# A written-out order of 1,999 operations: the same operations, all behind the first 278 in a newly drawn order

## The chip, the core and the metric

One core of one Trainium2 chip runs the whole kernel. The metric is the time of one execution in device microseconds, as the median of several runs. The profile is that of one execution, taken by the hardware profiler; it has a time of its own, and the span from its first to its last recorded event is somewhat shorter.

The engines are named as in the profile: PE (TensorE, matrix products), DVE (VectorE), ACT (ScalarE), POOL (GpSimd) and SP, whose queue issues most DMA transfers. Each engine works through its own queue in order. An instruction that waits holds up all that stands behind it in that queue.

## The reference

Attention over blocks of keys that each query selects, then a gated feed-forward layer. Four batches, eight heads, 768 positions of 64 features; 3,072 tokens, 512 features, 1,536 hidden ones.

```python
k_min, k_max = np.min(k_chunks, axis=3), np.max(k_chunks, axis=3)      # chunks of 32 keys
ub = sum_d max(q * k_min, q * k_max)                                   # a bound for each chunk
ub = np.where(causal, ub, -1e9)
top_chunks = np.argsort(ub, axis=-1)[..., -6:]
scores = q @ k.T / sqrt(64), masked to the top chunks and to earlier keys
attn = softmax(scores) @ v
x = attn as (3072, 512)
out = (sigmoid(x @ w_gate) * (x @ w_val)) @ w_out
```

## The kernel before, in words

The kernel describes its work as 1,999 named operations. `Plan.add` takes for each its engines, what it reads and writes, and the code that emits its instructions. A text, `ORDER`, then lists all names once. `Plan.order` reads it word by word: `name@ENGINE:slots` gives the engine (without `@`, the first of those that the operation allows) and the slot of every buffer that the operation is the first to hold. The instructions are emitted in that order, so the words of one engine, in their order, are that engine's queue, and a buffer that gets an occupied slot has to wait until the last reader of its former owner is done. The order between words of different engines has no effect by itself. Words are counted from 0 here.

The tokens are cut into units of up to three blocks of 128 queries. Unit u0 takes the first blocks of three batches, which need no selection; u1 to u7 the rest. For each unit:

- Loads. q and k of batch 0 come as wide tiles; for batches 1 to 3 as four transfers each (`load_blocks`, L568: k00, k01, k10, k11 and the same for q, 384 KB each), into one of two buffers of the kind `big`. v comes as one transfer per block (L581) into six buffers. A buffer is free for the next batch when all that reads it is done.
- Keys (L754): for each pair of heads p, `kx0`, `kx1` take minimum and maximum, `k16` casts, `kt` transposes, `hk0`, `hk1` spread the halves. Queries: `qf` transposes on DVE (L781), `qm` takes the positive part, `hq0`, `hq1` cast.
- Selection (L802): `ub` computes the bounds on PE, `ubn` transposes them, `mx` finds the sixth largest, `ap` compares, `apt` transposes back, and `hqm` copies the result into the rows of the query tile that carry the mask.
- Attention (L860): `sc` are score products in up to three banks per head, `exp` the exponential on ACT, `cm` the causal mask (POOL or DVE), `pv` the product with v, `rz` and `x` the normalisation on DVE. `xT` turns x by a DMA transpose on SP's queue (from u3 on; before by `xps` on PE).
- Feed-forward (L953) for u0 to u3: `g` and `v` products of four matmuls each, `tanh` on ACT, `hg` on DVE, three groups `o0`, `o1`, `o2` per block, `osb` and the store `out`.
- The units 4 and 5, and 6 and 7, are taken as pairs (`ffn_pair`, L1039; `project_pair`, L1185), with seven products where eight would be plain. `Sg`, `Sv`, `So` are sums of weights, `T0` to `T3` of inputs; `P1` to `P7` are the products, `E` copies a bank, `C` adds a bank to the copy, `hg` gates; `S1` to `S4` are sums for the output side, on DVE or POOL, `Q1` to `Q7` its products, `F` and `G` bring them into the output tile. This is called the pair stage below.

PSUM has eight banks, given out by the slots of the kind `ps`. `beat` are filler transposes on PE at the start.

Of the kernel before, what the change touches and what calls it, by code (L numbers as in the profile page):

```python
# [102 lines left out]
qT_u1_3:6 kxf1:1 kf1_1 hk1_u1_3@ACT hq0_u1_1@POOL k2_u2 qf_u1_2 vf1_1:1 kn_u1_2@DVE:0 beat3:7 qfT_0:2 qf_u1_3 qf0_1:0
kxf0 kT_u1_2:1 hq0_u1_3@POOL qf1_1 qf16_0:4 v10 qm_u1_2@ACT:0 vf_1:0 hk0_u1_1 qf_u1_0 after4 qf_u2_3@DVE:1 kf16_0:0
kcr_f kx0_u1_3 hkq101@POOL vf_2:1 beat4:7 scf_0:0,4,1 after2 vf1_3:2 kfT_1:3 expf_0_1:2 kn_u2_2@DVE:4 expf_0_0 hkf1
kx0_u1_2 beat5:7 kT_u2_2:4 qf0_2:3 kx1_u1_3 kf16_1:3 q2_u2 ident16 qm_u1_3@ACT beat6:7 qfT_1:0 cmf_0_0@DVE qf1_2
v16_0_0@ACT cmf_0_1@DVE kx1_u1_2 qf16_1:4 kf1_2:0 beat7:7 pvf_0_0:3 hq0_u1_0 rzf_0_0:0 k1_u2 beat8:7 scf_1:0,5,1
xf_0_0:0 kx1_u2_2:1 kf0_2 expf_1_0 xpsf_0_0:3,0 kt_u1_2@DVE:0 k3_u2 after6 expf_1_1:3 vf1_2:3 hk0_u1_3 k0_u2
qm_u1_0@ACT after5 vc_1@DVE wv0 qm_u1_1@ACT kx0_u2_2 q1_u2 hq1_u2_3 hk0_u1_2@POOL v_0_3:2 hkf0@ACT beat9:7 qfT_2:5 wg0
cmf_1_0@DVE pvf_0_1:1 v_0_2:1 xTf_0_0@ACT qn_u2_2@DVE:0 qf16_2@DVE:4 kn_u2_1:5 wg1 beat10:7 qT_u2_2:3 pvf_1_0:0  # L110
cmf_1_1@DVE beat11:7 kfT_2:5 kcr_u1 wv1 rzf_1_0:0 xf_1_0:0 kf16_2:0 rzf_0_1:1 wg2 hkq010 kn_u2_3:6 xf_0_1:1 beat12:7
scf_2:5,0,1 pvf_1_1:2 hk1_u1_2@POOL ub_u1:1,6 expf_2_1:2 rzf_1_1:1 wv2 xf_1_1:2 expf_2_0 cmf_2_1@DVE vc_2@ACT
cmf_2_0@DVE xpsf_1_1:5 xpsf_1_0:2 kT_u2_1:0 hq1_u1_2@POOL ubn1_u1:0 qf_u2_2 pvf_2_0:7 v_0_1:0 qm_u2_2@ACT:0 xpsf_0_1:3
hq1_u1_1@POOL rzf_2_0:1 pvf_2_1:6 xTf_1_0@ACT kx0_u2_1 kt_u2_2:0 kn_u2_0@POOL:3 xf_2_0:1 beat13:2 kT_u2_3:2 qn_u2_1:5
rzf_2_1:0 wo0 xTf_1_1@ACT xpsf_2_0:7 xf_2_1:0 kt_u2_1:1 qn_u2_0@DVE:6 beat14:4 xpsf_2_1:6 xTf_0_1@ACT ubn0_u1
qT_u2_1:5 hq0_u1_2@POOL xTf_2_0@ACT qT_u2_0:4 kx0_u2_3 xTf_2_1@ACT v_u0_2:1 hkp111@POOL kx1_u2_3 hkp000@ACT vb_u0_2
kt_u2_3@DVE:2 v_u0_1:6 ubm0_u1 mx0_u1:0 hk0_u2_3@POOL vb_u0_1 hkp010@ACT v_u0_0:2 wo1 vb_u0_0 ap0_u1 v_u0_3:7
# [5 lines left out]
sc_u1_3_1:3,3 tanh_u0_7 g_u0_5:6,3,6 kx0_u2_0 tanh_u0_6 kx1_u2_0 sc_u1_2_0:5 hq1_u1_3@DVE tanh_u0_5 kcr_u2@POOL
kt_u2_0@DVE:2 exp_u1_3_1 v16_0_3@DVE hq1 apt1_u1 hg_u0_2 g_u0_4:7,0,7 sc_u1_3_2:6 v_u0_6:0 v_u0_7:3 hqm1_u1_0 v_u0_4:2
tanh_u0_4 hg_u0_7 hq1_u1_0@POOL exp_u1_2_2 v_u0_5:7 exp_u1_2_0 hg_u0_4 hq1_u2_2 ub_u2:4,3 cm_u1_2@DVE exp_u1_3_2
hg_u0_5 hkq110@ACT sc_u1_3_0:7 ubn1_u2:0 g_u0_10:6,3,8 exp_u1_3_0 hqm1_u1_2@DVE g_u0_11:3,0,9 hg_u0_6 ubn0_u2
g_u0_8:0,1,10 mx0_u2:0 sc_u1_1_1:4 g_u0_9:7,2,11 exp_u1_1_1 ap0_u2 v16_0_2@DVE v_u0_8:4 tanh_u0_9 kcr1 apt0_u2:0
# [20 lines left out]
kt_1_2:0 qf16_3:4 sc_u2_5_0:5,1 v_u1_1:1 exp_u2_4_1 x_u2_0:0 g_u1_5:3,0,1 exp_u2_5_0 qf0_u3_0:1 kf16_3:3 sc_u2_5_1:2
hk1_1_0@DVE sc_u2_3_1:5 k11_2 v_u1_5:0 vc_3 qf0_u3_1 exp_u2_3_1 qf0_u3_2 sc_u2_5_2:6 exp_u2_4_2 v_u1_6:5 qf0_u3_3
exp_u2_5_1 xps_u2_0:7 cm_u2_5@DVE v_u1_8:4 tanh_u1_5 qm_u3_0@POOL:0 qf0_u4_2:0 k00_2 qm_u3_2@ACT hg_u1_5 pv_u2_3:3  # L150
pv_u2_2 exp_u2_5_2 xT_u2_0 qf0_u4_1 g_u1_6:7,0,2 hg_u1_8 hk1_1_1 scf_3:6,0,3 rz_u2_1:0 pv_u2_4:4 x_u2_1:0 expf_3_0
k10_2 pv_u2_5 g_u1_1:3,3,3 expf_3_1:0 cmf_3_0@DVE rz_u2_2:0 ub_u3:6,2 cmf_3_1 qf0_u4_3 tanh_u1_1 x_u2_2:1 tanh_u1_6
hq1_u3_0@POOL hg_u1_1 hk1_1_3@ACT v_1_2:0 hg_u1_6 pvf_3_1:7 pvf_3_0:1 hk1_1_2 xps_u2_1:4 o0_u1_0:3,0 rzf_3_1:0
out_u0_2 xf_3_1:0 rzf_3_0:1 hk0_1_2 v_2_1:2 ubn0_u3:0 o1_u1_0 qf0_u4_0 ubm0_u3 k16_2_0@ACT:0 xf_3_0:2 k16_2_3:2
q01_2:0 o2_u1_0 xT_u2_1 mx0_u3:0 k16_2_2@ACT:5 hq0_u3_2@POOL xpsf_3_1:4 o0_u1_1:1,1 ubn1_u3 ap0_u3 xps_u2_2:2 ubm1_u3
v16_1_2 xpsf_3_0:6 apt0_u3:0 o1_u1_1 xT_u2_2@ACT xTf_3_1 xTf_3_0@ACT hq0_u3_0@POOL mx1_u3 hqm0_u3_0@ACT o2_u1_1 q10_2
# [1252 lines left out]
```

## Time and profile before

| | us |
|---|---|
| median of three runs | 282.03 (281.38 to 282.8) |
| the profiled execution | 282.25 |
| its span | 280.2 |
| PE busy | 268.8 |
| DVE busy | 246.8 |
| ACT busy | 220.4 |
| POOL busy | 134.6 |

A row of the stretches gives, for each engine, its busy microseconds and in brackets its instructions. In the timeline a row has its start, its length, the engine, the line and what is written from what; what stands in square brackets at its end is how long the engine had been idle before and what it had waited for. "x4" at the end of a row of the chain or the timeline means that four instructions that follow each other were merged. PE's matmuls overlap, so a matmul's own length is longer than the step from one to the next.

### The profile page before, as it was taken

To read this page: it belongs to the slowest core of one execution; us is meant where nothing else is said; L and a number is where in the kernel's file an instruction comes from. 1 tells how busy PE (TensorE), PEld (TensorE's weight loads), DVE (VectorE), ACT (ScalarE), POOL (GpSimd) and SP (SyncE) were. 2 spreads that over 40 slices of the span, in tenths; PEclk is the share of its full clock that TensorE was granted. 3 is DMA by queue.
4 is the path that set the end of the run, shared out by engine and by line. 5 is a ranking of instruction groups with operands and counts; after the bars stand their busy time and mean duration, and the time that the engine had idled before them with its cause. 6 is when DMAs were issued, how large, how long until landed. Compare 5 with 4: busy or idle time off the path is not lost.

```text
span 280.2 us, 7449 instructions
## 1 busy us (share of the span) xinstructions
PE 268.8 (96%) x2758; PEld 186.3 (67%) x2758; DVE 246.8 (88%) x679; ACT 220.4 (79%) x474; POOL 134.6 (48%) x206
## 2 busy tenths in 40 slices
...
PEclk9999999999999999999999999999999999999999
...
DMA packets 131699, 34.68 MB, mean 124 GB/s; under 512 B 119760, under 2 KB 128720, under 8 KB 131664
## 3 DMA queue, kind: packets, MB, share of 16 engines
...
HBM read 30.67 MB, written 6.29 MB: 132 GB/s over the span
## 4 chain that ended last, share of the span: by engine, by line
PE 83%; DVE 5%; ACT 4%; DMA 3%; issue 2%; SPq 1%; POOL 0%; ACTq 0%; DVEq 0%
PE sc_u L876 12%; PE g_u L968 11%; PE v_u L968 10%; PE o_u L1006 10%; PE pv_u L912 6%; PE suo_u6u L1233 3%; PE suo_u4u L1233 3%; PE sug_u4u L1092 3%; PE suv_u4u L1092 3%; PE sug_u6u L1092 2%; PE suv_u6u L1092 2%; PE ube_u L814 2%; DMA k<-in_k_dram 2%; DMA kq_u<-in_q_dram 1%; PE sro_u4u L1233 1%
## 5 line engine op out<-in xcount | busy, mean ns | idle before, releaser
L887 ACT ACTIVATE att_u<-sc_u 128x512 f16<-128x512 f32 (+3 forms) x184 | 90.9, 549 | 15.1 <-PE sc_u L876 12.7
L896 POOL TENSOR_SCALAR_AFFINE_SELECT att_u<-att_u 128x384 f16<-128x384 f16 (+1 forms) x48 | 26.8, 570 | 44.0 <-ACT att_u L887 42.8
L968 PE MATMUL g_u<-xT_u,wg 128*128 128x384 f16 (+2 forms) x208 | 37.6, 314 | 0.0
L968 PE MATMUL v_u<-xT_u,wv 128*128 128x384 f16 (+2 forms) x208 | 36.4, 313 | 0.0
L1006 PE MATMUL o_u<-wo,hg_u 128*128 128x512 f16 x144 | 35.3, 379 | 0.1
L876 PE MATMUL sc_u<-hqe,hke 128*128 128x128 f16 (+2 forms) x220 | 28.2, 243 | 1.6 <-ACT hqe L359 1.2
L987 DVE SCALAR_TENSOR_TENSOR hg_u<-gate_u,v_u 128x384 f16<-128x384 f16 x48 | 24.8, 538 | 4.7 <-PE v_u L968 3.1
L912 PEld LDWEIGHTS <-att_u 128*128 128x128 f16 x640 | 25.0, 98 | 5.0 <-issue 1.2
L876 PE MATMUL sc_u<-hqo,hko 128*128 128x128 f16 (+2 forms) x220 | 27.9, 243 | 0.0
L912 PE MATMUL pv_u<-v,att_u 128*128 128x65 f16 x640 | 27.0, 193 | 0.0
L982 ACT ACTIVATE gate_u<-g_u 128x384 f16<-128x384 f32 x48 | 22.7, 498 | 5.0 <-PE g_u L968 3.3
L968 PEld LDWEIGHTS <-wv 128*128 128x128 f16 x208 | 19.1, 98 | 10.1 <-issue 0.5
L968 PEld LDWEIGHTS <-wg 128*128 128x128 f16 x208 | 18.9, 98 | 9.5 <-issue 0.2
L876 PEld LDWEIGHTS <-hke 128*128 128x128 f16 x220 | 16.6, 98 | 8.9 <-issue 1.9
L1006 PEld LDWEIGHTS <-hg_u 128*128 128x128 f16 x144 | 13.2, 98 | 11.9 <-issue 0.7
L876 PEld LDWEIGHTS <-hko 128*128 128x128 f16 x220 | 17.0, 98 | 5.8
L931 DVE TENSOR_TENSOR x_u<-pv_u,rz_u 128x384 f16<-128x384 f32 (+1 forms) x28 | 15.0, 534 | 1.2 <-DMA xT_u<-x_u 0.4
L365 POOL CAST v<-v 128x512 f16<-128x512 f32 x15 | 9.1, 612 | 12.9 <-DMA v<-in_v_dram 9.4
L480 PE MATMUL beat<-ident 128*128 128x128 f32 x70 | 12.0, 305 | 1.4 <-POOL ident masks.py:199 1.4
L837 DVE MAX8 mx_u<-ubn_u 128x8 f32<-128x8 f32 (+16 forms) x152 | 12.7, 159 | 0.1
L1092 PEld LDWEIGHTS <-Sg 128*128 128x128 f16 x96 | 9.0, 98 | 5.2
L1092 PEld LDWEIGHTS <-Sv 128*128 128x128 f16 x96 | 9.0, 98 | 5.0 <-issue 0.3
...
## 6 DMA issues: line engine op xcount, KB each, us to landing
...
k<-in_k_dram SPq DMA_DIRECT2D x12, 384.0 KB, 5.7
q<-in_q_dram SPq DMA_DIRECT2D x12, 384.0 KB, 5.8
...
```

The costliest lines, as they stand in the source:

```text
L837: nc.vector.max(at(mx)[:, e_, j, :], at(ubn)[:, e_, j, 0:max(8, u.seen[j])])
L876: nc.tensor.matmul(at(t)[:, o:o + 128 * m], hk[b % 2][e_][:, p, 128 * jb:128 * jb + 128], hq[u.side][e_][:, p, 128 * x:128 * (x + m)], sta ...
L887: plan.add(f"exp_{u.name}_{h}_{y}", {ACT: act(n)}, lambda e, t=t, att=att, b0=b0, n=n: nc.scalar.activation(at(att)[:, b0:b0 + n], at(t), ...
L896: nc.gpsimd.affine_select(out=dv, in_=dv, compare_op=ALU.is_ge, fill=0.0, base=0, pattern=[[0, u.m], [1, 128]], channel_multiplier=-1)
L912: nc.tensor.matmul(at(pv)[:, last, x, :], at(att)[:, c:c + 128], v16[b % 2][:, jb, h, :], start=(jb == 0), stop=(jb == ib))
L931: plan.add(f"x_{u.name}_{p}", {DVE: dve(u.t)}, lambda e: nc.vector.tensor_tensor(at(x_).rearrange("p a (e d) -> p e a d", e=2), at(pv)[:, ...
L968: nc.tensor.matmul(at(t)[:, lo:hi], w16[:, c, 128 * fb:128 * fb + 128], at(u.xt)[:, c, lo:hi], start=(c == 0), stop=(c == 3))
L982: plan.add(f"tanh_{u.name}_{fb}", {ACT: act(T)}, lambda e, g=g, gate=gate: nc.scalar.activation(at(gate), at(g), AF.Tanh, scale=0.5), read ...
L987: plan.add(f"hg_{u.name}_{fb}", {DVE: dve(T)}, lambda e, w_=w_, gate=gate, hg=hg: nc.vector.scalar_tensor_tensor(at(hg), at(gate), 1.0, at ...
L1006: nc.tensor.matmul(at(o), hgs[c][1][1]()[:, 128 * tb:128 * tb + 128], wo16[:, fc, lo:hi], start=(c == 0), stop=(c == NFB - 1))
L1092: nc.tensor.matmul(at(t), left[i](c), right[i](c), start=first and c == 0, stop=c == 1, skip_group_check=not first)
L1233: nc.tensor.matmul(at(t), sums[what[i][0], f][1]()[:, 128 * tb:128 * tb + 128], what[i][1](f), start=first and f == 0, stop=f == half - 1, ...
```

## The change

Only the text `ORDER` differs. It has the same 1,999 names. On each engine the queue is the same up to word 278 or so; there the first difference on PE stands at its 71st operation. Behind it the order is drawn anew, with other engines for 132 operations and other slots for the buffers that 597 words give out. Some lines of it, those with the words that are spoken of:

```diff
--- before.py
+++ after.py
@@ -95,193 +95,194 @@
 BEATS = (14, 9, 4, 3, 8, 1, 3, 2, 1, 10, 2, 1, 4, 2, 2, 4)
 
 ORDER = """
-ident q3_u1:0 epat0:0 k0_u1 tri0 ap1 epat q2_u1 k1_u1 q3_u2:1 q1_u1 q0_u1 kn_u1_0:0 qn_u1_3@DVE:1 ap0 v11 kf1_0:0
...
-exp_u1_5_1 exp_u1_6_0 sc_u1_4_2:2,0 sc_u1_6_1:3 cm_u1_6@DVE k01_1 sc_u1_7_1:4,2 exp_u1_4_2 sc_u1_7_0:6 rz_u1_0:0
...
-kt_1_0:1 v_u1_3:3 cm_u2_7 q11_1:0 sc_u2_6_2:4 g_u1_3:0,0,9 kx0_1_1 hk0_1_0 exp_u2_6_2 v_u1_4:7 tanh_u1_3 kx1_1_3
...
-g_u1_11:7,2,6 hg_u1_2 hg_u1_3 sc_u2_3_2:4,2 v_u1_11:6 exp_u2_3_2 kx1_1_1 tanh_u1_11 qfT_3:3 q10_1 sc_u2_3_0:4 hg_u1_11
...
-exp_u3_6_1 ap0_u4 exp_u3_5_2 v_u2_9:0 k01_3 hq0_u4_0@POOL apt0_u4:0 tanh_u2_9 v_u2_5:3 tanh_u2_10 hg_u2_9 hk1_2_0
...
-sc_u4_2_1:2,0 ub_u5:7,0 k16_3_3@ACT:2 k16_3_2:0 v_2_5:4 hg_u2_10 hg_u2_8 out_u1_2 hqm0_u4_0@ACT hq1_u5_2@POOL pv_u3_4
...
-o2_u3_0 cm_u5_6 exp_u5_4_2 ap1_u6 ub_u7:1,0 exp_u5_4_1 rz_u5_1:1 cm_u5_4 x_u5_1:1 osb_u3_0 hqm0_u6_2 apt1_u6 xT_u5_1
...
-C3g_u4u5_4 P4g_u4u5_5 E0v_u4u5_5:3 P5v_u4u5_4 C0v_u4u5_4 tanh_u4u5_0_11:1 P6v_u4u5_4 cm_u7_7 C0v_u4u5_5 P4g_u4u5_4
...
-P4v_u6u7_4 S4_u6u7_2@POOL hg_u6u7_0_11 Q1_u6u7_1:5,0,7,0 hg_u6u7_0_10 Q1_u6u7_2:1,6,2 C1v_u6u7_4 F0_u6u7_1
...
-F2_u6u7_1 out_u7_1 Q3_u6u7_1 G3_u6u7_0 Q4_u6u7_0 G1_u6u7_1 out_u6_1 F2_u6u7_0 out_u7_0
...
+ident q3_u1:0 epat0:0 k0_u1 beat0:7 tri0 epat q2_u1 ap1 k1_u1 q3_u2:1 q1_u1 qn_u1_3@DVE:1 q0_u1 kn_u1_0:0 ap0 v11
...
+g_u0_7:3,1,4 hq1_u1_0@DVE ap1_u1 hg_u0_1 kT_u2_0:6 sc_u1_3_1:4,2 apt1_u1 hq1_u1_3@POOL kcr1 gb_u0_2 tanh_u0_2 hg_u0_2
...
+k16_1_0@ACT:5 q01_1:0 kf0_3 q00_1 sc_u2_7_0:4 o0_u0_2:1,1 v_u1_5:3 hg_u1_5 o1_u0_2 o2_u0_2 hq0_u2_3 v16_0_5
...
+g_u1_1:1,0,9 exp_u2_2_2 x_u2_0:0 sc_u2_5_2:2 v_u1_1:6 k16_1_2:4 hk1_1_1 kt_1_2:1 q11_1 qf0_u4_2:1 tanh_u1_1 hg_u1_1
...
+kcr_2@POOL tanh_u2_3 hg_u2_3 pv_u3_0:2 ub_u4:4,0 ubn0_u4:0 k00_3:1 qf0_u5_0 pv_u3_1 hk1_1_2@ACT tanh_u2_9
...
+hg_u2_5 k16_3_2@ACT:1 sc_u3_4_1:6 exp_u3_4_1 xT_u3_0:0 v_1_5:3 cm_u3_6 hqm0_u4_0 pv_u3_7:3 v_u2_6:2 k16_3_0@ACT:5
...
+o2_u3_0 cm_u5_7 pv_u5_7 cm_u5_4 pv_u5_4:4 xT_u5_0:0 out_u2_2 x_u5_1:2 xT_u5_1 mx0_u7:0 exp_u6_0_1 Sv1 v16_2_5@DVE Sv3
...
+exp_u6_4_0 o2_u3_2 osb_u3_2 T0_u4u5:0 hk1_3_1@DVE cm_u6_1@DVE ap0_u7 pv_u6_1:0 P5g_u4u5_1:4 mx1_u7 E3g_u4u5_1:6
...
+S2_u4u5_0 hg_u4u5_0_5 P4g_u4u5_4 tanh_u4u5_0_10:0 tanh_u4u5_0_4:2 P3v_u4u5_5 C1v_u4u5_5 cm_u7_2 pv_u7_2:7
...
+tanh_u6u7_1_10:0 P2v_u6u7_5 C0v_u6u7_5 P7g_u6u7_5 C3g_u6u7_5 hg_u6u7_0_5 P5v_u6u7_4 S1_u6u7_3@POOL S3_u6u7_3@POOL
...
+tanh_u6u7_1_11:1 hg_u6u7_1_11 S1_u6u7_4 S1_u6u7_5 Q1_u6u7_1:6,0,1,0 Q1_u6u7_2:3,5,4 F0_u6u7_2 S2_u6u7_4 S4_u6u7_1
...
+S4_u6u7_4 S4_u6u7_5 Q6_u6u7_0 S3_u6u7_5 F3_u6u7_2 F1_u6u7_0@DVE S4_u6u7_3@POOL Q3_u6u7_2 F1_u6u7_2@DVE G1_u6u7_2
...
+out_u6_1 Q4_u6u7_0 F2_u6u7_0@DVE out_u7_0
 """
```

More of the change, by code (lines that the diff above doesn't have):

```diff
@@ L103 @@
[L103 to L117, printed above, removed]
@@ L123 @@
[L123 to L127, printed above, removed]
@@ L148 @@
[L148 to L156, printed above, removed]
-hk0_1_3 kx1_2_0:1 g_u2_4:6,0,12 osb_u1_1 ap1_u3 sc_u3_0_2:4,0 sc_u3_0_0:2 apt1_u3 tanh_u2_4 v_u2_3:1 hqm0_u3_2@DVE
```

322 lines of the change are left out of this document (175 added, 147 removed).

## The prediction

> **What bounds the kernel now.** I read the page first, then the span in seven stretches, then the chain of waits and the timeline at the one stretch that is not full.
>
> ```profile
> span 280.2 us, 7449 instructions
> PE 268.8 (96%) x2758; PEld 186.3 (67%) x2758; DVE 246.8 (88%) x679; ACT 220.4 (79%) x474; POOL 134.6 (48%) x206
> PEclk9999999999999999999999999999999999999999
> PE 83%; DVE 5%; ACT 4%; DMA 3%; issue 2%; SPq 1%; POOL 0%; ACTq 0%; DVEq 0%
> ```
> ```profile
> core 0: us, PE busy (x) PEld busy (x) DVE busy (x) ACT busy (x) POOL busy (x), PEclk, DMA share, GB/s
> 0.00:35.00 35.00, 28.99 (x286) 23.49 (x287) 28.01 (x92) 26.91 (x56) 24.59 (x53) 1.00 1.01 211
> 35.00:120.00 85.00, 84.96 (x890) 55.24 (x889) 74.70 (x221) 66.20 (x141) 37.70 (x60) 1.00 1.04 185
> 120.00:130.00 10.00, 8.35 (x82) 4.16 (x81) 8.94 (x16) 6.42 (x11) 5.39 (x8) 1.00 0.70 150
> 130.00:167.47 37.47, 37.47 (x466) 25.94 (x464) 34.81 (x116) 34.16 (x72) 27.12 (x38) 1.00 0.62 130
> 167.47:212.90 45.43, 45.22 (x512) 30.54 (x512) 43.08 (x111) 43.30 (x95) 21.95 (x30) 1.00 0.13 34
> 212.90:276.80 63.90, 63.78 (x531) 46.94 (x528) 57.28 (x128) 43.00 (x103) 17.85 (x22) 1.00 0.14 48
> 276.80:280.20 3.40, 0.00 (x0) 0.00 (x0) 0.00 (x0) 0.38 (x1) 0.00 (x0) 0.87 0.40 154
> ```
>
> The profiled execution took 282.25 us, 2.05 us outside its span of 280.2; it stands 0.22 us above the median of the three runs, 282.03. TensorE carries 83% of the chain at a full clock. Beyond 35 us it is idle for 0.04 + 1.65 + 0.21 + 0.12 us by these rows, then 3.4 us while the last output leaves. Busy time hides part of a loss, since matmuls overlap in it, so I also count work by steps. The chain gives a step where TensorE follows itself:
>
> ```profile
> 71.46 0.65 PE v_u L968 x4
> 126.66 0.86 PE o_u L1006 x4
> 218.50 0.66 PE suo_u4u L1233 x6
> ```
> ```profile
> L968 PE MATMUL g_u<-xT_u,wg 128*128 128x384 f16 (+2 forms) x208 | 37.6, 314 | 0.0
> L968 PE MATMUL v_u<-xT_u,wv 128*128 128x384 f16 (+2 forms) x208 | 36.4, 313 | 0.0
> L1006 PE MATMUL o_u<-wo,hg_u 128*128 128x512 f16 x144 | 35.3, 379 | 0.1
> L912 PE MATMUL pv_u<-v,att_u 128*128 128x65 f16 x640 | 27.0, 193 | 0.0
> ```
>
> That is 0.163 us for 384 columns, 0.216 for 512, 0.110 for 256, or 0.42 ns a column. With the counts (352 full-width products of L968, 336 of 384 columns in the pair products P, 144 of L1006, 252 of 256 columns in the pair projections Q, 640 of L912 at 0.030, 440 score matmuls of together 82,000 columns, seven bounds at about 1.2 us) the work after 35 us is about 235 us. It stands in 276.8 - 35 = 241.8 us. So some 6.5 us is all that any order of this work could win there, and the largest single piece is here:
>
> ```profile
> 118.57 5.43 DMA k<-in_k_dram
> 124.17 0.78 issue
> ```
> ```profile
> 123.58 1.03 PE L1006 MATMUL o_u<-wo,hg_u 128*128 128x512 f16 x4
> 124.10 0.83 ACT L359 CAST k<-k 128x768 f16<-128x768 f32 x1 [3.03 <-DMA k<-in_k_dram]
> 124.94 0.83 ACT L359 COPY hqe<-apt_u 64x768 f16<-64x768 f16 x1
> 125.83 0.22 PE L876 MATMUL sc_u<-hqe,hke 128*128 128x128 f16 x1 [1.22 <-ACT hqe L359]
> 126.45 0.22 PE L876 MATMUL sc_u<-hqe,hke 128*128 128x128 f16 x1 [0.41 <-ACT att_u L887]
> ```
>
> The last quarter of batch 3's keys, k01_3, is issued at 118.57 and lands at 124.0. ScalarE's cast k16_3_3 stands in front of it for 3.03 us, and behind the cast stands hqm0_u4_0, which the score matmul at 125.83 needs. The projection before it ends its steps at 123.58 + 0.86 = 124.44, so TensorE loses 1.39 us, and 0.57 more ahead of 126.45 (125.83 + 0.05 to 126.45): **2.0 us**.
>
> **What the change does, and what each part costs.** It removes and adds no operation; TensorE's first 70 operations stay, which is 35 us. After that every queue is redrawn, 132 operations change engine and 597 their buffers. I added the durations of before along each queue: TensorE's work stays 258.1 us by steps, DVE's goes from 246.1 to 243.4, ACT's from 219.1 to 213.2, POOL's from 134.6 to 140.9. None passes TensorE in the sum, so the sums alone give no change; what counts is where one queue runs late.
>
> *The wait for k_3: -2.0 us (between 0 and -2.0).* In the new order the four loads follow kx1_2_0, which frees their buffer after 87.7 us of TensorE work, only out_u1_2 between them waiting until 92.6; their first reader k16_3_2 stands at 102.5. The margin is 9.8 to 14.7 us, where before it was 8.4 for k01_3 (released at 101.2 behind v16_2_0, used at 109.6). A load takes
>
> ```profile
> k<-in_k_dram SPq DMA_DIRECT2D x12, 384.0 KB, 5.7
> q<-in_q_dram SPq DMA_DIRECT2D x12, 384.0 KB, 5.8
> ```
>
> to land, so four at half a microsecond of issue each need about 7.7. I take the whole gain.
>
> *A new wait for q_1: +0.3 us (0 to 1.3).* The last loads of batch 1's queries now stand behind qf0_3, which waits for v16_0_4 at 54.8; DVE's qf0_u4_2 wants them at 61.2, a margin of 6.4. Before, the same loads went out like this:
>
> ```profile
> 69.72 0.42 SPq L552 DMA_DIRECT2D qf<-in_q_dram  x1
> 71.17 4.82 SPq L573 DMA_DIRECT2D q<-in_q_dram  x3
> ```
>
> Four issues (qf0_3, q10_1, qf1_3, q11_1) at 0.42 to 0.5 us and 5.8 to land make 7.7: DVE stands some 1.3 us late. Queued behind it are hg_u1_1, four more transposes of q and hg_u1_3. The first TensorE operation that needs one of them is sc_u2_2_1 at 66.0, whose bank hg_u1_1 frees, 4.4 us after hg_u1_1's turn, and DVE has 10 us idle of the 85 before 120. That is the cover; without it the 1.3 us would pass on.
>
> *DVE in the pair stage: +1.1 us (0 to 3.5).* From word 1205 to 1580 (150.8 to 195.2 us of TensorE work) DVE's queue now holds 93 instructions and 45.0 us against 91 and 44.0 before, for the same 44.3 us of TensorE. It gains Sv1, So0, So1, C0v, C1v, a net E, one hg, two cm, two S2, v16_2_5 and hk1_3_1 and gives up Sg0, Sv2, apt1_u6, ubn0, ubn1, an x, two rz and three S3:
>
> ```profile
> L1034 DVE TENSOR_TENSOR Sv<-wv 128x1536 f16<-128x1536 f16 x2 | 1.9, 949 | 0.0
> L1180 DVE TENSOR_TENSOR hko<-wo 128x1536 f16<-128x1536 f16 x1 | 1.0, 952 | 0.0
> L1107 DVE TENSOR_TENSOR c0v_u4u<-c0v_u4u,sqv_u4u 128x384 f32<-128x384 f32 x6 | 3.2, 546 | 0.0
> L848 DVE STREAM_TRANSPOSE apt_u<-ap 128x384 f16<-128x384 f16 (+2 forms) x14 | 7.3, 522 | 0.3
> L825 DVE STREAM_TRANSPOSE ubn_u<-ubo_u 128x384 f32<-128x384 f32 (+2 forms) x7 | 3.7, 534 | 1.2 <-PE ubo_u L814 1.1
> L931 DVE TENSOR_TENSOR x_u<-pv_u,rz_u 128x384 f16<-128x384 f32 (+1 forms) x28 | 15.0, 534 | 1.2 <-DMA xT_u<-x_u 0.4
> ```
>
> Before, DVE was busy for 43.08 of the stretch's 45.43 us, so a microsecond more on it lengthens the stretch by up to 1.055. I take 1.0 x 1.055. Nothing, if its idle 2.35 us can be used; 3.5, if POOL's 27.4 us there (22.6 before) hold DVE up besides. What such a hold-up looks like before:
>
> ```profile
> L1122 DVE SCALAR_TENSOR_TENSOR hg_u<-gate_u4u,c0v_u4u 128x384 f16<-128x384 f16 x6 | 3.7, 625 | 0.0
> L1122 DVE SCALAR_TENSOR_TENSOR hg_u<-gate_u4u,suv_u4u 128x384 f16<-128x384 f16 x6 | 3.1, 542 | 0.0
> ```
>
> The form that reads its second input from a c tile takes 83 ns more than the one that reads it from a bank. Eight such microseconds of hg, and eight of T, S, cm and weight sums, are 16 of DVE's 45; if that share of POOL's added 4.8 us were lost to DVE it would be 1.7 us, and with the order's own 0.95 to 1.5 us the bound is (1.7 + 1.5) x 1.055 = 3.4, rounded up.
>
> [...]
>
> *Closer spacing elsewhere: +1.0 us (0 to 1.6).* Adding each queue's durations up to the operation that makes an input, and TensorE's steps up to the one that needs it, 89 TensorE operations before have their last input less than 0.2 us ahead of their turn; in the new order 120. The 4.5 us that before loses beside k_3 come to 0.05 us for each of the 89, 1.6 us for 31 more; part lies in the pair stage and is counted there.
>
> *The end: nothing.* The last projections (word 1936 on) follow each other as before, and the way out after the last matmul is the same 3.4 us. New there are four sums on POOL (S2 and S4 of columns 0 and 3):
>
> ```profile
> L1215 POOL TENSOR_TENSOR hgp_u<-hg_u,hgp_u 128x384 f16<-128x384 f16 x6 | 5.6, 929 | 8.7 <-DVE v L1215 8.7
> ```
>
> With S1 and S3 of column 3 ahead of them they are six of 0.93 us from 240.8 on, done at 246.4, and their first reader Q6_u6u7_2 stands at 250.2. The 3.8 us between hide them; without, each would cost its 0.93.
>
> Sum: -2.0 + 0.3 + 1.1 + 1.0 = +0.4 against 282.25: 282.65, or 282.4 by the median; I write **282.6**.
>
> **Rivals.**
> 1. *Slower: DVE sets the end of the pair stage.* Place: words 1205 to 1580; price 3.5 in place of 1.1, so 285.0, and 287 if the k_3 gain is lost to another load as well. For it: DVE 95% busy there already, more work given to it and to POOL. Against: ACT gets 1.0 us less there, and behind it DVE has 4.8 us less work than TensorE (58.1 to 62.9). It decides from 2.3 us of delay on (283.7).
> 2. *Faster: the k_3 wait goes and the rest is absorbed.* 282.25 - 2.0 = 280.2; for it the margins of the other block loads (12.5 us and more but for q_1) and the lighter DVE and ACT; against it that TensorE has no slack to hide anything in. Getting half of the 4.5 us besides would make 278.
> 3. *The redraw does nothing:* queues that only change places in words. The engines and buffers that differ speak against it; 282.0.
>
> **How the numbers follow.** Forecast 0.38, rival 1 0.32, rival 2 0.28, rival 3 0.02. Below 0.5% a measurement of this kernel, whose three runs lie 0.5% apart, can't tell a change from none. The forecast's own range is 281.0 to 284.2: 0.28 within 0.5%, 0.09 slower, 0.01 faster. Rival 1 gives 0.31 slower and 0.01 same; rival 2 0.27 faster and 0.01 same. Together faster 0.28, same 0.32, slower 0.40. The range runs from 279.5, past rival 2, to rival 1's upper end at 287.
>
> **What would show it.** Right: no TensorE idle of more than 0.5 us with k behind it; DVE waiting about 1 us for q near 73 us without an idle TensorE after it; in the pair stage hg or c tiles as releasers of TensorE, 1 to 2 us in all. Wrong: any stretch before 150 us with over 1 us of idle TensorE, from a load with a margin that I held to be enough, or a pair stage over 48 us.

## The result, and the profile after

| | us |
|---|---|
| after, median of four runs | 287.01 (285.1 to 289.73) |
| before, in the same call | 281.73 (281.38 to 282.8) |
| ratio after to before | 1.0157 (95% interval 1.0122 to 1.0192) |
| the profiled execution of after; its span | 289.73; 288.0 |

The change makes the kernel 1.6% slower, which is 4.4 us. The ratio leaves out the slowest of the four executions, 289.73 us, which is the profiled one, so every reading below is also held against a second profile of the same kernel (e1_after_again: 286.09, span 284.3).

The page of after, first execution, with the same four lines as before:

```profile
span 288.0 us, 7460 instructions
PE 271.8 (94%) x2758; PEld 188.2 (65%) x2758; DVE 251.1 (87%) x679; ACT 215.5 (75%) x468; POOL 141.2 (49%) x212
PEclk9999999999999999999999999999999999999999
PE 77%; DVE 11%; DMA 4%; ACT 3%; issue 2%; SPq 1%; DVEq 0%; ACTq 0%
```

DVE's share of the chain has gone from 5% to 11%, TensorE's from 83% to 77% (10% and 79% in the second profile). Where in time that lies, the stretches of the second profile say, cut where TensorE has the same amount of its work behind it as at 35.0, 167.47, 212.9 and 276.8 us before (columns as before):

```profile
0.00:36.81 36.81, 30.91 (x286) 25.29 (x287) 28.64 (x93) 27.48 (x57) 25.26 (x53) 1.00 0.99 206
36.81:168.82 132.01, 131.01 (x1449) 84.86 (x1449) 115.35 (x347) 105.65 (x222) 75.05 (x111) 1.00 0.88 163
168.82:214.95 46.13, 45.32 (x471) 30.44 (x469) 44.90 (x105) 42.40 (x96) 24.14 (x31) 1.00 0.16 42
214.95:279.77 64.82, 64.23 (x556) 47.25 (x554) 60.14 (x137) 39.94 (x96) 16.81 (x19) 1.00 0.13 44
279.77:284.30 4.53, 0.00 (x0) 0.00 (x0) 0.42 (x1) 0.00 (x0) 0.00 (x0) 0.86 0.46 175
```

Before, these stretches took 35.0, 132.47, 45.43, 63.9 and 3.4 us. So the head, up to the first redrawn matmul, is 1.8 us longer, the wait of that matmul, 0.7 us, included; the next part is 0.5 shorter, although the 2.0 us that the prediction counted for the wait for k_3 are gone from it, so some 1.5 are given back there; the pair stage is 0.7 longer and the part behind it 0.9; the way out of the last output 1.1. In the first profile the middle three are the same within 0.2 us (131.85, 46.13, 64.82), but the head takes 40.63 and the way out 4.57. That is the first thing to settle: the head's queues are the same, instruction for instruction, in both kernels.

TensorE's waits behind 36 us, for the first profile of after (engine, line, what it waited for: us in total, times, longest):

```profile
PE g_u L969 <- ACT gate_u L983: 0.5, 1, 0.5
PE sc_u L877 <- DVE x_u L932: 0.4, 1, 0.4
PE v_u L969 <- ACT gate_u L983: 0.4, 1, 0.4
PE sc_u L877 <- DVE c1v_u4u L1108: 0.4, 1, 0.4
PE sc_u L877 <- DVE c0g_u4u L1108: 0.3, 1, 0.3
PE kT_u L714 <- DVE hg_u L988: 0.2, 1, 0.2
PE sc_u L877 <- ACT gate_u L983: 0.2, 1, 0.2
```

and for the profile of before:

```profile
PE sc_u L876 <- ACT hqe L359: 1.2, 1, 1.2
PE sc_u L876 <- ACT att_u L887: 0.4, 1, 0.4
```

Before, one late load makes both rows. After, the load is gone from the list and seven places of 0.2 to 0.5 us stand in its stead, each behind a tanh on ACT or a gating, an addition or a normalisation on DVE. This view counts idle time only; counted by steps, as in the prediction, each place costs 0.1 to 0.2 us more (g_u0_7: 0.71).

### The profile page after: what moved, and what is told of

Same layout as the page of the kernel before. It is cut to its first block, busy times and chain, and to the rows that moved or that the text cites. A ratio compares the mean times of both kernels' runs of the same rounds, so it can differ in the third digit from the quotient of the medians.

```text
span 288.0 us, 7460 instructions
## 1 busy us (share of the span) xinstructions
PE 271.8 (94%) x2758; PEld 188.2 (65%) x2758; DVE 251.1 (87%) x679; ACT 215.5 (75%) x468; POOL 141.2 (49%) x212
## 4 chain that ended last, share of the span: by engine, by line
PE 77%; DVE 11%; DMA 4%; ACT 3%; issue 2%; SPq 1%; DVEq 0%; ACTq 0%
PE v_u L969 10%; PE sc_u L877 10%; PE g_u L969 10%; PE o_u L1007 9%; PE pv_u L913 5%; PE suo_u6u L1234 3%; PE suo_u4u L1234 3%; PE suv_u6u L1093 3%; PE sug_u6u L1093 3%; PE ube_u L815 2%; DMA kq_u<-in_k_dram 2%; PE sug_u4u L1093 2%; PE suv_u4u L1093 2%; PE sro_u6u L1234 1%; PE sro_u4u L1234 1%
## 5 line engine op out<-in xcount | busy, mean ns | idle before, releaser
L897 POOL TENSOR_SCALAR_AFFINE_SELECT att_u<-att_u 128x384 f16<-128x384 f16 (+1 forms) x47 | 24.6, 530 | 39.1 <-ACT att_u L888 38.5
L969 PE MATMUL v_u<-xT_u,wv 128*128 128x384 f16 (+2 forms) x208 | 37.3, 313 | 0.4 <-ACT gate_u L983 0.4
L988 DVE SCALAR_TENSOR_TENSOR hg_u<-gate_u,v_u 128x384 f16<-128x384 f16 x48 | 25.4, 537 | 7.2 <-PE v_u L969 4.4
L877 PE MATMUL sc_u<-hqe,hke 128*128 128x128 f16 (+2 forms) x220 | 27.1, 243 | 1.0 <-DVE x_u L932 0.4
L877 PE MATMUL sc_u<-hqo,hko 128*128 128x128 f16 (+2 forms) x220 | 27.2, 243 | 0.5 <-DVE c1v_u4u L1108 0.4
L1216 POOL TENSOR_TENSOR v<-hgp_u 128x384 f16<-128x384 f16 x5 | 4.7, 950 | 21.7 <-PE suv_u6u L1093 12.3
L481 PE MATMUL beat<-ident 128*128 128x128 f32 x70 | 13.0, 324 | 1.7 <-POOL ident masks.py:199 1.4
L366 POOL COPY hqe<-apt_u 64x768 f16<-64x768 f16 (+2 forms) x10 | 8.1, 812 | 11.2 <-DVE apt_u L849 10.8
```

The lines of the kernel that those rows point to most:

```text
L481: nc.tensor.transpose(at(beat), ident32, ident32)
L877: nc.tensor.matmul(at(t)[:, o:o + 128 * m], hk[b % 2][e_][:, p, 128 * jb:128 * jb + 128], hq[u.side][e_][:, p, 128 * x:128 * (x + m)], sta ...
L897: nc.gpsimd.affine_select(out=dv, in_=dv, compare_op=ALU.is_ge, fill=0.0, base=0, pattern=[[0, u.m], [1, 128]], channel_multiplier=-1)
L969: nc.tensor.matmul(at(t)[:, lo:hi], w16[:, c, 128 * fb:128 * fb + 128], at(u.xt)[:, c, lo:hi], start=(c == 0), stop=(c == 3))
L988: plan.add(f"hg_{u.name}_{fb}", {DVE: dve(T)}, lambda e, w_=w_, gate=gate, hg=hg: nc.vector.scalar_tensor_tensor(at(hg), at(gate), 1.0, at ...
```

## The experiments

Two numbers are read from each profile. The *head* ends where g_u0_2 starts, the last projection that stands at the same place in both orders; it follows the last four-matmul beat by 2.69 us in every profile. The *measure* runs from there to the end of the last matmul. What remains to the span's end is the *way out*, good to 0.05 us, since spans are given to 0.1. For e1_after_again: beat at 32.97, g_u0_2 at 35.66, last matmul 278.95 + 0.82 = 279.77, measure 244.11, way out 4.53.

| kernel | span | head | measure | way out | median of its runs | ratio to before |
|---|---|---|---|---|---|---|
| before | 280.2 | 34.60 | 242.19 | 3.40 | 281.73 | |
| e4_before_again | 280.3 | 35.76 | 241.18 | 3.37 | 282.37 (one) | |
| e2_before_k3 | 278.0 | 34.64 | 240.05 | 3.31 | 281.06 | 1.0005 (0.9959 to 1.0051) |
| e9_before_dve | 281.7 | 36.05 | 242.02 | 3.63 | 282.85 | 1.0036 (1.0001 to 1.0071) |
| after | 288.0 | 39.48 | 243.94 | 4.57 | 287.01 | 1.0157 (1.0122 to 1.0192) |
| e1_after_again | 284.3 | 35.66 | 244.11 | 4.53 | 285.86 | 1.0154 (1.0084 to 1.0224) |
| e3_E_act | 284.1 | 35.90 | 244.74 | 3.46 | 286.03 | 1.0161 (1.0097 to 1.0225) |
| e5_pool | 281.1 | 34.84 | 242.80 | 3.46 | 283.97 | 1.0108 (1.0082 to 1.0135) |
| e6_order | 284.7 | 35.75 | 244.83 | 4.12 | 286.16 | 1.0163 (1.0113 to 1.0214) |
| e7_all | 285.8 | 36.54 | 245.83 | 3.43 | 287.10 | 1.0185 (1.0120 to 1.0250) |
| e8_mended | 279.6 | 34.49 | 241.62 | 3.48 | 282.22 | 1.0030 (0.9993 to 1.0066) |
| e10_So0 | 280.3 | 34.55 | 242.30 | 3.45 | 284.20 | 1.0101 (1.0060 to 1.0141) |
| e11_light | 281.9 | 34.71 | 243.72 | 3.47 | 283.27 | 1.0079 (1.0039 to 1.0119) |

And where TensorE loses the measure's time: its start less the work ahead of it by steps, by five stretches of its own work (21 us is g_u0_2, 150 to 195 the pair stage, 195 to 225 what follows it; "by steps" means that a start is compared with the sum of the usual distances from one matmul to the next):

| lost, us | 21 to 120 | 120 to 150 | 150 to 195 | 195 to 225 | 225 to end | sum |
|---|---|---|---|---|---|---|
| before | 4.12 | 0.68 | 1.15 | 0.05 | 0.68 | 6.68 |
| e4_before_again | 2.70 | 1.09 | 1.15 | 0.06 | 0.67 | 5.67 |
| e2_before_k3 | 1.87 | 0.80 | 1.15 | 0.05 | 0.66 | 4.53 |
| e9_before_dve | 1.87 | 1.92 | 1.40 | 0.66 | 0.67 | 6.52 |
| after | 3.54 | 1.36 | 1.77 | 1.35 | 0.41 | 8.43 |
| e1_after_again | 3.54 | 1.52 | 1.77 | 1.36 | 0.40 | 8.59 |
| e3_E_act | 3.53 | 1.35 | 3.11 | 0.82 | 0.41 | 9.22 |
| e5_pool | 3.70 | 0.80 | 1.43 | 0.96 | 0.40 | 7.29 |
| e6_order | 3.56 | 0.80 | 3.19 | 1.37 | 0.40 | 9.32 |
| e8_mended | 2.45 | 0.91 | 1.41 | 0.95 | 0.39 | 6.11 |
| e10_So0 | 2.46 | 0.79 | 0.96 | 2.17 | 0.40 | 6.78 |
| e11_light | 3.26 | 1.19 | 1.58 | 1.78 | 0.40 | 8.21 |

**Is the head's loss the kernel's? e1_after_again and e4_before_again.** Both kernels are unedited.

> The changed kernel once more, unedited. In its first profile the part whose order did not change (up to the projection g_u0_2) ended 4.9 us later than before (39.48 against 34.60 us), the redrawn part lost 1.8 us on TensorE after it and the way out of the last output 1.2 us. Theory chance: the 4.9 us belong to that one execution; here g_u0_2 starts at 34.6 to 36.5 us, the span is 282 to 285 us, and the redrawn part again loses 1.5 to 2 us on TensorE. Theory kernel: something in the changed kernel makes its head slow in every execution; g_u0_2 starts at 38 us or later, the span is 286 us or more. Ratio of times by the first 1.005 to 1.015, by the second 1.02 and more.

> The kernel before once more, unedited, for a second profile. Theory chance: its head varies as the changed kernel's does, so g_u0_2 starts anywhere from 34.6 to 38 us. Theory kernel: g_u0_2 starts at 34.3 to 35.0 us again.

The head of after ends at 35.66 this time, that of before at 35.76. The timeline of TensorE, first of before, then of before once more, of after, and of after once more, shows two beats each, the nine matmuls of the second beat and the last four:

```profile
6.36 1.15 PE L480 MATMUL beat<-ident 128*128 128x128 f32 x9
31.91 0.61 PE L480 MATMUL beat<-ident 128*128 128x128 f32 x4
```
```profile
6.60 2.13 PE L480 MATMUL beat<-ident 128*128 128x128 f32 x9
33.06 0.61 PE L480 MATMUL beat<-ident 128*128 128x128 f32 x4
```
```profile
6.99 2.13 PE L481 MATMUL beat<-ident 128*128 128x128 f32 x9
36.79 0.61 PE L481 MATMUL beat<-ident 128*128 128x128 f32 x4
```
```profile
6.60 2.13 PE L481 MATMUL beat<-ident 128*128 128x128 f32 x9
32.97 0.61 PE L481 MATMUL beat<-ident 128*128 128x128 f32 x4
```

The same nine matmuls take 1.15 us or 2.13, in either kernel; where they take 1.15 the head ends between 34.49 and 34.84 (six profiles), where they take 2.12 or 2.13 between 35.66 and 39.48 (seven). The spread is made before the third beat: from there (9.17 us in before, 10.34 in e4_before_again) it is 25.4 to 25.7 us to the head's end in twelve of the thirteen profiles. The theory chance holds for the head. In the first profile of after this part takes 28.65 us. Part of that is a late load, a row that the head's waits of the other three do not have; the rest stays open:

```profile
PE kfT L626 <- DMA kf<-in_k_dram: 1.6, 1, 1.6
```

The expectation's span of 282 to 285 us was met (284.3), its ratio of 1.005 to 1.015 was just missed (1.0154): the 244.11 us from g_u0_2 on, the same as in the first profile within 0.2, belong to the kernel.

**The wait for k_3: e2_before_k3.** Of this and the following diffs the words that matter are shown, some of them gathered from several lines of ORDER.

```diff
-hk1_2_1 k10_3 hg_u2_0
+hk1_2_1 k10_3 k01_3 hg_u2_0
...
-exp_u3_5_2 v_u2_9:0 k01_3 hq0_u4_0@POOL apt0_u4:0
+exp_u3_5_2 v_u2_9:0 hq0_u4_0@POOL apt0_u4:0
```

> The kernel before with one word moved: the load k01_3 stands straight behind k10_3 in SyncE's queue, ahead of xT_u3_1, v_1_5 and v_2_2. My step on k_3 says that TensorE loses 2.0 us around 124 to 126.5 us for this load: the time falls by 1.5 to 2.0 us (280.0 to 280.5), ratio 0.993 to 0.995, and no TensorE idle over 0.5 us with k behind it is left. The rival, that the next wait stands right behind it, gives 0 to -0.7 us.

In the profile the step is right: the whole list of TensorE's waits behind 36 us is one row,

```profile
PE suv_u4u L1092 <- DVE c1v_u4u L361: 0.2, 1, 0.2
```

with a head as fast as before's (34.64) the measure falls by 2.14 us and the span by 2.2. The time shows no gain: 1.0005 of before, where 0.993 to 0.995 was expected; the interval leaves room for 1.2 us at most. The second profile of the unedited kernel says why. There k01_3 is not waited for at all:

```profile
PE pv_u L912 <- POOL v L365: 0.6, 1, 0.6
PE pv_u L912 <- DVE osb_u L1016: 0.2, 1, 0.2
```

The load left at 119.11 instead of 118.57, but TensorE stood 2 us further back, 1.2 us by its head and 0.8 by a wait of pv_u1_2 at 51.0 us for a cast of v on POOL. So the wait takes what TensorE has not lost already. It is no constant of the kernel; the 13 runs of before beside this one go down to a span of 277.6, and so do those of e2_before_k3.

**DVE's load, taken to ScalarE: e3_E_act.**

```diff
-E0v_u4u5_0@DVE:3 E1v_u4u5_0@DVE:5 E1v_u4u5_3@DVE:0 E3v_u4u5_3@DVE:6 E3g_u4u5_4@DVE:4
+E0v_u4u5_0:3 E1v_u4u5_0:5 E1v_u4u5_3:0 E3v_u4u5_3:6 E3g_u4u5_4:4
```

> The changed kernel with five evictions of the pair stage (E0v and E1v of column 0, E1v and E3v of column 3, E3g of column 4) back on ScalarE, where the kernel before has them: DVE has 2.35 us less to do there, ScalarE 2.35 us more. If DVE sets the end of the pair stage (rival 1), TensorE's losses of 2.0 us between 183 and 230 us of the changed kernel's trace fall by 1 to 2 us and the time is 1 to 2 us below the changed kernel's in this call. If ScalarE, as full as DVE there, takes over, or the loss lies in single late inputs, the time changes by less than 0.5 us.

The loss behind the stage falls by 0.5 (1.36 to 0.82), that inside it rises by 1.3 (1.77 to 3.11). Two of its waits are new:

```profile
PE pv_u L913 <- DVE c0g_u4u L1108: 0.5, 1, 0.5
PE sc_u L877 <- ACT att_u L888: 0.4, 1, 0.4
```

ScalarE, busy for 42.4 of the stage's 46.1 us before this edit, takes over. The time, 286.03 beside 285.86 us, is as the second theory had it; the measure is 0.63 us longer. DVE, busy for 44.9 us of the same 46.1, and ACT are full together.

**DVE's load, taken to POOL, and the converse: e5_pool, e9_before_dve.**

```diff
-hk1_3_1@DVE cm_u6_1@DVE cm_u6_3@DVE S2_u4u5_0 S2_u4u5_1
+hk1_3_1@POOL cm_u6_1@POOL cm_u6_3@POOL S2_u4u5_0@POOL S2_u4u5_1@POOL
```

> The changed kernel with five short operations of the pair stage (hk1_3_1, cm_u6_1, cm_u6_3, S2 of columns 0 and 1) on POOL, where the kernel before has them: DVE has 1.6 us less to do there, and ScalarE's work stays. Measure: TensorE from the start of g_u0_2 to the end of its last matmul, 243.95 and 244.11 us in the two profiles of the changed kernel, 240.05 in that of the kernel before with k01_3 moved. If DVE's load is what TensorE loses 1.4 us to between 203 and 230 us, the measure falls by 0.8 to 1.4 us (to 242.7 to 243.3). If POOL in its turn takes time from DVE, it falls by less than 0.4 us.

The measure falls by 1.31, and the ratio to before from 1.0154 to 1.0108, with intervals that overlap. The number of the first theory (0.8 to 1.4) is met, but by luck: 0.72 of the 1.31 lie between 120 and 150 us, ahead of all five operations. There v_u3_8 waits for a tanh behind a chain on DVE, in the first three profiles of this order and not here. In e1_after_again the chain is late from a normalisation on that needs its buffer back from a transposing transfer, a row that waits less in e5_pool:

```profile
143.39 0.56 DVE L932 TENSOR_TENSOR x_u<-pv_u,rz_u 128x384 f16<-128x384 f32 x1 [1.08 <-DMA xT_u<-x_u]
```
```profile
141.90 0.56 DVE L932 TENSOR_TENSOR x_u<-pv_u,rz_u 128x384 f16<-128x384 f32 x1 [0.26 <-DMA xT_u<-x_u]
```

In the first profile of after this normalisation waits for nothing; there the causal mask behind it takes 0.98 us beside a copy on POOL, where it takes 0.35 in the other two:

```profile
146.83 0.83 POOL L366 COPY hqe<-apt_u 64x768 f16<-64x768 f16 x1
146.89 0.98 DVE L895 TENSOR_TENSOR att_u<-att_u,tri 128x384 f16<-128x384 f16 x1
```

0.74 us is what the five operations themselves gave, just below the forecast: 0.34 in the stage, 0.40 behind it.

The converse puts the same five on DVE in the order of before, with k01_3 moved as in e2_before_k3:

```diff
-hk1_3_1 cm_u6_1 cm_u6_3 S2_u4u5_0@POOL S2_u4u5_1@POOL
+hk1_3_1@DVE cm_u6_1@DVE cm_u6_3@DVE S2_u4u5_0@DVE S2_u4u5_1@DVE
```

> The converse of e5_pool: the kernel before with k01_3 moved (as in e2_before_k3, measure 240.05 us) and the same five short operations, hk1_3_1, cm_u6_1, cm_u6_3 and S2 of columns 0 and 1, on DVE as the change has them; DVE has 1.6 us more to do in 45 us, of which it idled 2.35. If DVE's load has a price of its own whatever the order, the measure rises by 0.8 to 1.4 us, to 240.9 to 241.5. If it costs only where DVE is already late by the order, it rises by less than 0.4 us.

Beside e2_before_k3 the measure rises by 1.97, more than either theory said; the ratios, 1.0036 and 1.0005, lie within each other's intervals. Half of the 1.97 is one place: hk1_3_1, 0.81 us, now stands ahead of hg_u3_6, whose bank a score product needs.

```profile
PE sc_u L876 <- DVE hg_u L987: 0.9, 1, 0.9
PE sug_u4u L1092 <- DVE c3g_u4u L1107: 0.2, 1, 0.2
```

0.25 more is lost in the stage and 0.61 behind it. The loss behind the stage, 0.05 or 0.06 in the other three profiles of the order of before, comes with these operations, and in the order of after it goes in part without them.

**The order alone: e6_order.** On ScalarE qm_u6_0 goes behind tanh_u3_8, on DVE Sv1 and Sv3 behind x_u5_2.

```diff
-qf1_u6_1 qm_u6_0@ACT:0 o0_u2_2:6,0
+qf1_u6_1 o0_u2_2:6,0
...
-tanh_u3_8 qf1_u6_2
+tanh_u3_8 qm_u6_0@ACT:0 qf1_u6_2
...
-exp_u6_0_1 Sv1 v16_2_5@DVE Sv3
+exp_u6_0_1 v16_2_5@DVE
...
-x_u5_2:0 sc_u6_3_1:6
+x_u5_2:0 Sv1 Sv3 sc_u6_3_1:6
```

> The changed kernel with three words moved: on ScalarE qm_u6_0 behind tanh_u3_8, on DVE Sv1 and Sv3 behind x_u5_2. No work changes its engine. Theory (single late inputs): the gaps of 0.6 to 0.7 us ahead of v_u3_8 and of 0.61 us ahead of sc_u6_3_1 go, and the measure from g_u0_2 to the last matmul falls by 0.9 to 1.3 us from 244.1. Rival (DVE is the bound from 165 us on, whatever its order): the second gap comes back at the next operation that DVE feeds, and the measure falls by 0.5 to 0.7 us.

The first edit takes away the loss at v_u3_8 (1.52 to 0.80, though e5_pool shows that it can be missing without an edit). The second takes away the wait at sc_u6_3_1 and loses 1.4 us:

```profile
PE srg_u4u L1093 <- DVE Sg L1035: 0.9, 1, 0.9
PE g_u L969 <- ACT gate_u L983: 0.5, 1, 0.5
PE suv_u4u L1093 <- DVE c0g_u4u L1108: 0.5, 1, 0.5
```

Sv1 and Sv3 had filled time in which x_u5_3 waited for its product anyway. Behind it they delay Sg3. The measure rose by 0.72 where both theories expected it to fall; the time did not move (1.0163).

**The seam: e6_seam, e7_all, e8_mended.** g_u0_7, the first redrawn matmul, waits 0.71 us for bank 3, which tanh_u0_1 reads; kT_u2_0 behind it waits 0.39 for hg_u0_1. In e6_seam banks 1 and 3 change names from there on; e7_all has that, the edit of e6_order and that of e5_pool.

```diff
-g_u0_2:5,0,3 qm_u2_0@ACT exp_u1_0_2 qm_u2_1 tanh_u0_1
-g_u0_7:3,1,4 hq1_u1_0@DVE ap1_u1 hg_u0_1 kT_u2_0:6 sc_u1_3_1:4,2 apt1_u1 hq1_u1_3@POOL kcr1 gb_u0_2
+g_u0_2:5,0,3 gb_u0_2 qm_u2_0@ACT exp_u1_0_2 qm_u2_1 tanh_u0_1
+g_u0_7:1,1,4 sc_u1_3_1:4,2 g_u0_6:7,2,5 hq1_u1_0@DVE ap1_u1 hg_u0_1 kT_u2_0:6 apt1_u1 hq1_u1_3@POOL kcr1
...
-v_u0_7:1 exp_u1_0_0 hg_u0_7 v_u0_6:2 v_u0_4:3
+v_u0_7:3 exp_u1_0_0 hg_u0_7 v_u0_6:2 v_u0_4:1
```

> The changed kernel with the first redrawn operations mended: banks 1 and 3 change names from g_u0_7 on, so that g_u0_7 does not wait for the bank that tanh_u0_1 still reads, and gb_u0_2, sc_u1_3_1 and g_u0_6 stand ahead of kT_u2_0, which waits for hg_u0_1. Theory (the redraw's losses are single late inputs): the two gaps of 0.71 and 0.39 us just behind the unchanged part go, and the measure from g_u0_2 to the last matmul falls by 0.8 to 1.1 us from 244.1. Rival (work is only shifted and the wait comes back within 10 us): by less than 0.3 us.

> The three edits of the runs beside it together. If their gains are those of separate late inputs they add: the measure from g_u0_2 to the last matmul falls by 2.5 to 3.5 us from 244.1, to 240.6 to 241.6, and the time comes within 1.5 us of the kernel before. If they share one bound (DVE behind 165 us), the sum of the single gains is 0.5 us and more above the joint one.

In e6_seam's profiled execution the granted clock was 0.56 and the span 463.3 us, so it stands in neither table and the forecast of its measure is untested. Its ratio to before is 1.0184 (1.0105 to 1.0263), no better than unedited. e7_all was to reach 240.6 to 241.6 us and took 245.83, more than the unedited order, and shows the edit to be bad:

```profile
PE g_u L969 <- DVE hg_u L988: 2.1, 1, 2.1
PE srg_u4u L1093 <- DVE Sg L1035: 1.1, 1, 1.1
```

Bank 1 still belongs to v_u0_2, until hg_u0_2 has read it, so g_u0_7 waits 2.3 us by steps instead of 0.71. Bank 2 is free from hg_u0_0 on. e8_mended uses it (banks 2 and 3 change names behind it), keeps the POOL edit and qm_u6_0 behind tanh_u3_8, and leaves Sv1 and Sv3 alone:

```diff
-g_u0_7:3,1,4 hq1_u1_0@DVE ap1_u1 hg_u0_1 kT_u2_0:6 sc_u1_3_1:4,2
+g_u0_7:2,1,4 sc_u1_3_1:4,2 g_u0_6:7,2,5 hq1_u1_0@DVE ap1_u1 hg_u0_1 kT_u2_0:6
```

> The changed kernel with three edits: the five short operations on POOL as in the run e5_pool; qm_u6_0 behind tanh_u3_8 on ScalarE (Sv1 and Sv3 stay where the change put them); and the first redrawn operations mended with bank 2, which is free from hg_u0_0 on, instead of bank 1, which v_u0_2 holds until hg_u0_2. Theory (single late inputs, and DVE's load in the pair stage): from 244.1 us the measure g_u0_2 to last matmul falls by 1.3 for POOL, 0.6 to 0.7 for v_u3_8 and 0.8 to 1.1 for the two gaps behind g_u0_2, to 241.0 to 241.6. If the waits come back later, it stays at 242.3 or more.

The measure is 241.62, 2.49 below e1_after_again, at the edge of the 2.5 to 3.1 forecast, and three rows of waits are left:

```profile
PE sc_u L877 <- DVE c0g_u4u L1108: 0.3, 1, 0.3
PE sc_u L877 <- DVE x_u L932: 0.3, 1, 0.3
PE sc_u L877 <- ACT gate_u L983: 0.2, 1, 0.2
```

The seam's loss is gone whole: from 21 to 25 us of TensorE's work 0.04 instead of 1.13. The time is 1.003 of before, with 1 inside the interval: the three edits together take back most of the 1.6%. What each gives in time was not run alone.

**Load or order: e10_So0, e11_light.** Both start from e8_mended. In e10_So0 the sum So1 is taken ahead of So0, which it reads, so its numbers are others.

```diff
-E0g_u4u5_5:3 So0 P6v_u4u5_3
+E0g_u4u5_5:3 P6v_u4u5_3
...
-hg_u4u5_1_5 sc_u7_4_0:0
+hg_u4u5_1_5 So0 sc_u7_4_0:0
```
```diff
-v16_2_5@DVE S2_u4u5_3 S4_u4u5_1 S4_u4u5_3
+v16_2_5@ACT S2_u4u5_3@POOL S4_u4u5_1@POOL S4_u4u5_3@POOL
```

> The run e8_mended with one word moved: the weight sum So0 (0.87 us on DVE) from ahead of C0g of column 5 to behind hg_u4u5_1_5, 13 us later, which is about where the kernel before has it; its first reader stands later still. TensorE's wait of 0.46 us for C0g of column 5 (at 204.3 us of that trace) goes in either case. Theory load (DVE works without a pause from 198 to 227 us, so it is its sum that counts): the same time is lost again at sc_u7_6_3 and P5v_u6u7_1, and the measure g_u0_2 to last matmul stays within 0.2 us of 241.62. Theory single late inputs: it falls by 0.4 to 0.5 us.

> The run e8_mended with four more operations taken off DVE in the pair stage: v16_2_5 back on ScalarE, S2 of column 3 and S4 of columns 1 and 3 on POOL; DVE has 1.2 us less there by the durations of before, 1.9 by that trace. Theory load: TensorE's remaining 1.95 us of loss between 165 and 230 us of the trace fall by 0.4 to 0.9 us, the measure from 241.62 to 240.7 to 241.2. Theory order (what is left are single late inputs that these four do not touch): it changes by less than 0.2 us.

Both theories missed both. In e10_So0 the wait for C0g of column 5 goes, but the measure rises by 0.68: P7v of column 4 now waits 0.84 us by steps for an eviction behind So0, which takes 1.66 us at its new place beside POOL's instructions, 0.95 at the old.

```profile
PE suv_u4u L1093 <- DVE c1v_u4u L362: 0.7, 1, 0.7
```
```profile
213.98 1.66 DVE L1181 TENSOR_TENSOR hke<-wo 128x1536 f16<-128x1536 f16 x1
```

In e11_light, with 1.2 us less work on DVE, the losses in the stage and behind it rise from 2.36 to 3.36 us, and 1.1 us more are lost ahead of the four edits, at places where nothing was edited. So from one profile the 1.0 us alone would prove little. The waits name hg and ACT's osb:

```profile
PE sc_u L877 <- DVE hg_u L1123: 0.7, 1, 0.7
PE sc_u L877 <- ACT gate_u L983: 0.5, 1, 0.5
PE sc_u L877 <- ACT osb_u L1016: 0.4, 1, 0.4
```

The timeline shows why hg is late. First e11_light, then e8_mended, the same hgp of column 4 and what POOL does beside it:

```profile
219.49 1.22 POOL L1216 TENSOR_TENSOR hqe<-hg_u,hqe 128x384 f16<-128x384 f16 x1
219.86 1.26 DVE L1123 SCALAR_TENSOR_TENSOR hgp_u<-gate_u4u,c3v_u4u 128x384 f16<-128x384 f16 x1
```
```profile
217.65 0.65 POOL L897 TENSOR_SCALAR_AFFINE_SELECT att_u<-att_u 128x384 f16<-128x384 f16 x1 [1.37 <-ACT att_u L888]
217.83 0.87 DVE L1123 SCALAR_TENSOR_TENSOR hgp_u<-gate_u4u,c3v_u4u 128x384 f16<-128x384 f16 x1
```

In e11_light it takes 1.26 us and ends 0.41 us after POOL's sum; in e8_mended it takes 0.87 and ends 0.40 us after POOL's mask. Another hgp, of column 5, takes 1.31 against 0.60. The two delays are 1.1 us; the one sum moved from DVE ahead of them saved 0.3.

No version here beats both kernels. e2_before_k3 and e8_mended come out level with before.

## Why the prediction was right and wrong

The result stands at the very end of the range of 279.5 to 287.0 and 4.4 us above the forecast of 282.6: at the upper end of rival 1, which was to need 3.5 us of DVE's delay and the k_3 gain lost besides. The first did not come: DVE's delay was 1.9 us. In the times the k_3 gain is missing, but it was not lost to another load, as the rival had it; the rest of the excess came from closer spacing, a term that the prediction held to 1.6 us at most. So that the range held is in good part luck. None of the prediction's own signs of being wrong appeared either: behind the head TensorE is nowhere idle for more than 0.6 us, and the pair stage took 46.13 us, not over 48. By the steps:

- **The wait for k_3 (-2.0).** The mechanism was right: behind the head no wait with k behind it is in either profile of after, and in e2_before_k3 the measure is 2.14 us below the profiled case. The step failed in what it was subtracted from. The prediction worked from one execution with a fast head, where the wait was long; in the second profile of before it was nil, and 10 runs without it show no gain (at most 1.2 us by the interval). The sum began with -2.0 and should have begun between -1.2 and 0. This and the spacing below are the two large errors.
- **A new wait for q_1 (+0.3).** Not there: no row of DVE's waits between 60 and 100 us has q in it. TensorE loses 0.56 us from 60 to 75 us of its work against 0.33 before, so +0.2.
- **DVE in the pair stage (+1.1, up to 3.5).** The bound held and the place was short. From 150 to 195 us of TensorE's work the loss rose by 0.62 (1.15 to 1.77); 1.3 more came behind it, from 195 to 225, where the prediction counted on DVE having 4.8 us less work than TensorE. Together 1.9, below the 2.3 from which rival 1 was to decide. For the five operations that stood on POOL before, the price is 0.7 of the 1.9 (e5_pool). Other work of DVE, taken to ACT, cost 0.8 us more there, not less (e3_E_act: 3.93 against 3.13 in the stage and behind it).
- **DVE held up by POOL (nothing in the +1.1, an estimated 1.7 in its bound of 3.5).** The prediction read such a hold-up from a mean of 83 ns, and in the value it counted nothing for it. That step failed. The 83 ns were the mean of six gatings of which five took 0.55 us and one, beside a sum on POOL, 1.02. In the pair stage of after, DVE's instructions with both inputs in SBUF took 2.8 us more than alone, eight of them, each beside POOL; before it was 0.9 us and three. DVE's busy time there rose by 1.8 (43.08 to 44.90 us), so the rise is this and not the 1.0 of added work. One of them is the weight sum Sg3, shown first of before, then of after's second profile:

```profile
176.19 0.95 DVE L1034 TENSOR_TENSOR Sg<-wg,Sg 128x1536 f16<-128x1536 f16 x1
```
```profile
180.34 0.93 POOL L366 COPY hqe<-apt_u 64x768 f16<-64x768 f16 x1
180.51 1.57 DVE L1035 TENSOR_TENSOR Sg<-wg,Sg 128x1536 f16<-128x1536 f16 x1
```

  In all 13 profiles together, none of the 827 such sums, masks and gatings without a POOL instruction beside them is over 4% longer than the median of its kind; of 317 with one, 154 are longer by 0.03 to 0.76 us. The 771 gatings with one input in a bank took at most 0.56 us, beside POOL or not. How much of TensorE's 1.9 us comes from it is not shown, since no run takes this delay alone away.
- **Closer spacing elsewhere (+1.0, up to 1.6).** Mis-sized, and beyond its bound: against e2_before_k3, which has no k_3 wait either, after loses 1.67 us more up to 120 (0.2 of it the row of q_1) and 0.56 to 0.72 from there to 150, so 2.0 to 2.2. 1.1 of it stands in two places at the seam, which a mean over 31 operations could not show; e8_mended takes them away whole. 0.56 to 0.72 is the wait of v_u3_8. The rest is spread: gaps of 0.15 to 0.4 us.
- **The end: nothing.** Right for TensorE: 0.40 lost behind 225 us against 0.66. The way out took 4.57 and 4.53 us in the two profiles of after, 3.43 to 3.48 in six of the seven others with the same last words, so it varies by run.
- **The head: 35 us, unchanged.** It is no constant: the same instructions took 34.49 to 39.48 us in 13 profiles.

Without the -2.0 the prediction's own terms sum to +2.4; after against e2_before_k3 lost 4.1 us by the measure (8.59 - 4.53). The 1.7 us between the two are 1.0 to 1.2 for the spacing, 0.8 for DVE and -0.1 for q_1. In time after lies 1.57% or 4.4 us above before, 1.54% in the second call, and before is level with e2_before_k3. So the losses on TensorE account for the time within the interval of 1 us. What varies between runs, the head and the way out, stays open as to the order: four of the nine profiles with the redrawn order had the fast head, two of the four with the order of before.
